# Keeping the second head group of a linear attention on chip, with VectorE sums and a new order of the seven products

## The chip, the cores and the metric

The kernel runs on one core of a Trainium2 chip. The metric is device time in microseconds (us) of one execution; lower is better. The engines have short names in the profile: PE is the matrix engine, PEld its weight loads, DVE the vector engine, ACT the scalar engine, POOL and SP the two engines that mostly issue DMAs here. Each engine works through its own instructions strictly in order and waits at semaphores for the others.

## What is computed

An input `x` of 2048 tokens by 512 goes through two branches, which a sigmoid gate mixes:

```python
g = sigmoid((x * gate_w).sum(-1))
# branch a: linear attention, 32 heads of 16
q, k, v = split(x @ wqkv)
pq, pk = phi(q), phi(k)          # phi(t) = (t+1 if t > 0 else exp(t)) + 1e-6
kv  = pk^T v      per head;   z = sum over tokens of pk
a = ((pq kv) / (pq z + 1e-6)) @ wo
# branch b: bilinear GLU, 1792 hidden columns
b = ((x @ w_gate) * (x @ w_up)) @ w_down
out = g * a + (1 - g) * b
```

## The kernel before

All matrices are float32. A product is made from three matmuls of rounded operands: `split` writes a high part (an ACT copy that rounds) and a low part (a DVE subtraction), and `mm3` adds high times high, high times low and low times high.

The first stage (to about 92 us) makes k, the sums over tokens, and per head block the small matrices kv. Then `kv` and `wo` are multiplied into one 512x512 matrix W', stored in DRAM in 256x256 blocks (`wraw`). So what the second stage calls **o** is the normalised `pq`, and branch a is o times W'.

The second stage runs over two **pairs** of token chunks (1024 tokens each). Each pair has 16 **units**: 14 for the hidden columns of branch b (`f`) and two for q (`q`), in the order f0 f1 f2 q f3 f4 f5 q f6 to f13 in the first pair and f0 q f1 f2 f3 q f4 to f13 in the second. They are counted through: units 0 to 15 and 16 to 31. A unit is a fast 2x2 block multiplication with seven products (products 2, 3, 4, 1, 5, 6, 7 in that order, six 512-wide matmuls each) into the PSUM banks Y, X, R and S. DVE and ACT combine the banks between the products (`bR`, `t`, `bS`, `cross`, `m`).

Between the products PE works off **down jobs** (h times `w_down`: six 512-wide matmuls each), as many at each of four places in a unit as the table `shares` says: after product 3, after product 4, after product 5, and before product 6. An entry `(0, 1, 0, 1)` gives one after product 4 and one before product 6. The first down job of each token tile is taken from PSUM by ACT (`acc<-att`, `acc<-dn`), the later ones by DVE.

Everything else is hung on named places of units with `later(n, place, fn)`: `e` (after product 3), `c` and `d` (after product 4), `t` (after product 1), `s` (after product 5), `r` (after product 6), `end` (after product 7). The order in which these calls run is the order on each engine, since every operation is pinned to program order.

**How o comes about.** A q unit makes one of two groups of heads (`j` = 0 or 1), in four parts of 128 rows by 512 tokens: row half r, token half c. `quad` writes phi(q) into a tile of the pool `ph`; the three units after that make the denominators, by way of DRAM (`terms`, `den`), and `norm_end` multiplies phi(q) by the scaled reciprocal that a broadcast DMA has put into a tile `rb` (pool `z`). `o_there` then stores the part to DRAM (`opark`), in a block named by group and token half: "11", "12", "21", "22".

**What is done with it.** `products` multiplies o by W' with seven block products (`OPROD`). Each entry holds: a number, the blocks of W' to be summed (one or two, a minus for a sign), the blocks of o to be summed, whether the product goes on in the PSUM bank of the one before, and which blocks of the result take it. Each product has two **steps** (one per half of the tokens); in the second pair the same seven products also take four units of branch b (`MIXED`, rows `hraw`), so that each has two steps for h and two for o. A step sits on one place: four per unit in the first pair, five in the second. Around step k, `load(k + 5)` fetches the first block of o from DRAM on SP's queue, `add(k + 3)` has POOL add the second block to it in a DMA (`dma_add`), after an ACT negation where the first has a minus, `ready(k)` splits the sum into the operands `oh` and `ol`, and `job(k)`, twelve 256-wide matmuls and one or two DVE sums into `acc`, follows in PE's order after the next down place. `w_raw`, `w_sum` and `w_split` do the same for the weights (`wraw`, `owh`, `owl`), and `lead` says how many steps ahead.

SP's queue holds, besides, the loads of the unit weights (`w_load`: `wr<-in_wgu`, for the unit three later) and of `w_down` (`wdr`), and waits at each until the buffer is free. POOL's queue holds the adding loads of the unit weights (`w_add`: `wr<-in_wgu_add`), which need ACT to have copied two parts of the tile first. During units 15 and 16 the operands of x for the second pair are reloaded one by one (`reload`): load after the last product that used them, for three of them a DMA add, then a split by ACT and DVE.

Operations recorded through the helpers have the helpers' lines: L72 matmuls, L78 ACT, L81 and L84 DVE, L102 DMAs of SP, L105 adding DMAs of POOL.

Of the kernel before, what the change touches and what calls it, by code (L numbers as in the profile page):

```python
# [49 lines left out]

OPROD = (
# [12 lines left out]
def gated_mix(ctx: ExitStack, tc, xt, xp, x, wqkv, wq, wq_add, wo, wgu, wgu_add, wdn, gate_w, out):  # L64
# [336 lines left out]
    def o_down():  # L401
        while ojobs and ojobs[0][0] < passed[0]:
# [154 lines left out]
    def wp_load():  # L557
        att["wv"] = two_by_two("wv")
        att["wo"] = [p2.tile([P, D], F32, tag="ph", name="wo_sb", bufs=4) for _ in range(KT)]
        for k in range(KT):  # L560
            dma(att["wv"][k], wqkv[k * P:(k + 1) * P, 2 * D:3 * D])
        for k in range(KT):
            dma(att["wo"][k], wo[k * P:(k + 1) * P, :])
# [91 lines left out]
    def down_jobs(pair, group):  # L655
# [3 lines left out]
        def job(i):  # L659
# [28 lines left out]
            if not todo[0]:  # L688
# [5 lines left out]

    opark = {(p, b): dram.tile([2, P, 2, HALF], F32, name=f"opark{p}{b}") for p in range(NPAIR)
             for b in ("11", "12", "21", "22")}

    def attention(pair, j, n):
        phs, den = {}, {}
# [4 lines left out]
        def quad(r, c, q):  # L704
# [3 lines left out]
            ph = phs[r, c] = p2.tile([P, CH], F32, tag="ph", name="phq", bufs=4)  # L708
# [42 lines left out]
        def norm_end(i):  # L751
            r, c = parts[i]
            stt(den[i], phs[r, c], EPS, den[i], ALU.add, ALU.mult)
            o_there(f"{j + 1}{c + 1}", r, den[i])
# [13 lines left out]
        if j == 1:  # L768
            products(pair, n + 5)
# [6 lines left out]
    def products(pair, n0):  # L776
        raw, tiles, wt, bank = {}, {}, {}, {}
        steps = STEPS[bool(MIXED[pair])]
        step0 = len(steps) * n0 + (1 if MIXED[pair] else 2)


        lead = ((6, 3), (5, 3)) if MIXED[pair] else ((4, 2), (4, 2))
# [5 lines left out]

        def raw_tile(k):
            raw[k] = p2.tile([P, D], F32, tag=("z", "ph")[k % 2], name="oraw", bufs=4)  # L790
            return raw[k]

        def load(k):
            p, kind, i = line[k]
            if kind == "o":
                dma(raw_tile(k).rearrange("p (r t) -> p r t", r=2), opark[pair, OPROD[p][2][0][-2:]][i])

        def add(k):
            p, kind, i = line[k]
            if kind == "o":  # L800
                if len(OPROD[p][2]) == 2 and OPROD[p][2][0][0] == "-":
                    act(raw[k], raw[k], scale=-1.0)
                for block in OPROD[p][2][1:]:
                    dma_add(raw[k].rearrange("p (r t) -> p r t", r=2), opark[pair, block][i])

        def h_sum(k):
            p, kind, r = line[k]
            if kind == "h" and len(OPROD[p][2]) == 2:
                one, other = OPROD[p][2]
                tt(raw_tile(k), row(other, r), row(one, r), ALU.subtract if one[0] == "-" else ALU.add)  # L810
# [7 lines left out]
        def w_raw(j):  # L818
            p, kind, _ = line[2 * j]
            tag = ("z", "ph")[p % 2] if kind == "h" else "cb"  # L820
# [14 lines left out]
        def ready(k, place):  # L835
            p, kind, i = line[k]
            tiles[k] = hi, lo = o_tiles()
            src = raw.pop(k) if k in raw else row(OPROD[p][2][0], i)
            if OPROD[p][2] == ("-22",):
                act(hi, src, scale=-1.0)  # L840
                stt(lo, src, -1.0, hi.bitcast(F32), ALU.mult, ALU.subtract)
            else:
                split(hi, lo, src)
# [40 lines left out]
        def weights(k, ahead, fn):  # L884

            for j in range(last // 2):
                if 2 * j - 1 - (ahead and lead[j % 2][ahead - 1]) == k:
                    at_step(k, lambda place, j=j: fn(j))

        for k in range(-8, last):  # L890
# [3 lines left out]
            if 0 <= k + 1 < last:  # L894
                at_step(k, lambda place, k=k: h_sum(k + 1))
            if 0 <= k + 3 < last:
                at_step(k, lambda place, k=k: add(k + 3))
            weights(k, 2, w_sum)
            if 0 <= k + 5 < last:
                at_step(k, lambda place, k=k: load(k + 5))  # L900
# [157 lines left out]
```

## Time and profile before

| what | value |
|---|---|
| time, median of 3 runs | 606.84 us (606.51 to 607.49) |
| the profiled execution's own time | 606.07 us |
| its span, first to last instruction | 604.4 us |
| PE busy | 595.6 us (99%) |
| DVE busy | 461.9 us (76%) |
| ACT busy | 331.9 us (55%) |
| POOL busy | 76.3 us (13%) |
| moved by DMA | 113.94 MB |

All times in the profile are us from the start of the span. A group row reads: line, engine, operation, what it writes and reads, shape, count; then busy time, the mean of one in ns, and the idle time ahead of it with what ended it. A row of the timeline reads: start, duration, engine, line, operation, and in brackets the idle time before it with its releaser. A row of a windows table gives, for a stretch of time, its length and each engine's busy time, then the granted share of the PE clock (1.00 is full), the busy share of the 16 DMA engines and GB/s. Matmuls are pipelined: one takes 0.39 us from start to end, but the next may start after 0.23 us.

### The profile page before, as it was taken

The numbers are of one execution on the slowest core, as the hardware profiler recorded it, in microseconds if no ns is written. First come the engines' busy times: TensorE is split into PE (matmuls) and PEld (weight loads), VectorE is DVE, ScalarE is ACT, GpSimd is POOL, SyncE is SP. The second block draws the span as 40 slices with busy tenths as digits, with TensorE's granted clock in tenths as the row PEclk, the third lists the DMA queues.
The fourth block names the chain that finished last, engine by engine and source line by source line (L and its number), as shares of the span: only waits on it lengthen the run. The fifth ranks groups of instructions, "written<-read, shape, count | busy, mean of one in ns | idle before, by whom it ended". The sixth has DMA issues, their size and how long they took to land.

```text
span 604.4 us, 8314 instructions
## 1 busy us (share of the span) xinstructions
PE 595.6 (99%) x2898; PEld 497.8 (82%) x2898; DVE 461.9 (76%) x736; ACT 331.9 (55%) x580; POOL 76.3 (13%) x95
## 2 busy tenths in 40 slices
PE   9999999999999999999999999998999999999997
PEld 6888888888888878888888888786888798888886
DVE  6977896756787769777789976866587887878866
ACT  3855766579654744445455648459543556246330
POOL 0011100000011110222011221000102412201100
PEclk9999999999999999999999999999999999999999
DMA  9576949656869877999679957877679987935103
GB/s 296 175 196 124 297 89 294 158 154 177 250 151 241 204 206 196 253 262 226 187 163 237 227 158 194 220 210 187 145 191 254 231 203 196 233 60 123 21 16 139
DMA packets 63626, 113.94 MB, mean 189 GB/s; under 512 B 7840, under 2 KB 27808, under 8 KB 63520
## 3 DMA queue, kind: packets, MB, share of 16 engines
q1 hardware_dynamic: 50640, 75.40, 38.2%
q0 software_dynamic: 12656, 37.49, 34.8%
q10 hardware_dynamic: 288, 0.52, 0.3%
q8 instruction: 22, 0.36, 0.2%
q14 instruction: 20, 0.16, 0.1%
HBM read 97.65 MB, written 17.84 MB: 191 GB/s over the span
## 4 chain that ended last, share of the span: by engine, by line
PE 83%; DMA 7%; DVE 5%; issue 2%; ACT 2%; SPq 0%; DVEq 0%; POOL 0%; ACTq 0%; POOLq 0%
PE dn L72 14%; PE att L72 13%; PE bY L72 12%; PE bR L72 11%; PE bX L72 11%; PE pk L72 7%; PE gt L72 7%; PE bS L72 6%; DMA wr<-in_wgu 2%; DMA wraw<-in_wdn 1%; DMA zt<-terms 1%; DMA wdr<-in_wdn 1%; DMA den<-den 1%; PE warm L72 1%; DMA rb<-den 1%
## 5 line engine op out<-in xcount | busy, mean ns | idle before, releaser
L72 PE MATMUL dn<-slot,slot 128*128 128x512 f32 (+1 forms) x336 | 83.0, 386 | 0.0
L81 DVE TENSOR_TENSOR wcl<-wr,wch 128x512 fp32r<-128x512 f32 (+1 forms) x96 | 73.6, 773 | 1.9 <-ACT wch L78 1.7
L78 ACT ACTIVATE slot<-cross 128x512 fp32r<-128x512 f32 x48 | 30.2, 629 | 80.9 <-DVE cross L81 80.9
L72 PEld LDWEIGHTS dn<-slot,slot 128*128 128x128 f32 x336 | 61.7, 188 | 12.1
L72 PE MATMUL att<-slot,slot 128*128 128x512 f32 x246 | 62.3, 390 | 0.0
L78 ACT ACTIVATE wch<-wr 128x512 fp32r<-128x512 f32 (+1 forms) x96 | 60.4, 695 | 1.6 <-DMA wr<-in_wgu_add 1.6
L72 PEld LDWEIGHTS att<-slot,slot 128*128 128x128 f32 x246 | 45.8, 188 | 9.3
L105 POOL DMA_DIRECT2D wr<-in_wgu_add x28 | 24.1, 860 | 219.1 <-ACT wr L78 146.0
L72 PE MATMUL bX<-xbh,wch 128*128 128x512 f32 x128 | 49.8, 389 | 0.0
L72 PE MATMUL bX<-xbh,wcl 128*128 128x512 f32 x128 | 49.8, 389 | 0.0
L72 PE MATMUL bX<-xbl,wch 128*128 128x512 f32 x128 | 49.8, 389 | 0.0
L78 ACT ACTIVATE cross<-bY 128x512 f32<-128x512 f32 x32 | 19.1, 597 | 50.4 <-PE bY L72 50.2
L81 DVE TENSOR_TENSOR t<-bR,cross 128x512 f32<-128x512 f32 x32 | 22.1, 690 | 26.0 <-PE bR L72 14.0
L78 ACT ACTIVATE wr<-wr 128x512 f32<-128x512 f32 x64 | 36.7, 623 | 6.2 <-DMA wr<-in_wq 3.3
L84 DVE SCALAR_TENSOR_TENSOR acc<-dn,gate,acc 128x512 f32<-128x512 f32 (+1 forms) x45 | 33.1, 737 | 9.1 <-PE dn L72 8.8
L78 ACT ACTIVATE cross<-bX 128x512 f32<-128x512 f32 x32 | 19.1, 597 | 33.5 <-DVE bS L81 33.5
L81 DVE TENSOR_TENSOR bR<-bX,m 128x512 f32<-128x512 f32 x32 | 22.3, 698 | 18.4 <-PE bX L72 17.2
L84 DVE SCALAR_TENSOR_TENSOR acc<-att,gate,acc 128x512 f32<-128x512 f32 x36 | 26.9, 749 | 11.8 <-PE att L72 11.6
L81 DVE TENSOR_TENSOR slot<-cross,slot 128x512 fp32r<-128x512 f32 x48 | 32.8, 684 | 0.5
L78 ACT ACTIVATE m<-bY 128x512 f32<-128x512 f32 x32 | 19.1, 595 | 24.5 <-PE bY L72 24.4
L105 POOL DMA_DIRECT2D oraw<-opark x20 | 19.7, 1037 | 91.2 <-ACT oraw L78 27.8
L72 PE MATMUL att<-owh,ol 128*128 128x256 f32 x100 | 28.6, 286 | 0.7 <-DVE ol L81 0.7
(191 smaller groups left out, 1586.6 us busy)
## 6 DMA issues: line engine op xcount, KB each, us to landing
wr<-in_wgu_add POOLq DMA_DIRECT2D x28, 640.0 KB, 6.8
wr<-in_wgu SPq DMA_DIRECT2D x28, 384.0 KB
oraw<-opark SPq DMA_DIRECT2D x28, 256.0 KB
wdr<-in_wdn SPq DMA_DIRECT2D x24, 256.0 KB
oraw<-opark POOLq DMA_DIRECT2D x20, 256.0 KB, 6.3
xraw<-in_x SPq DMA_DIRECT2D x16, 256.0 KB
terms<-zq SPq DMA_DIRECT2D x16, 256.0 KB
zt<-terms SPq DMA_DIRECT2D x16, 256.0 KB
```

The costliest lines, as they stand in the source:

```text
L72: tc.keep_in_program_order(nc.tensor.matmul(*args, **kw))
L78: pin(nc.scalar.activation(dst, src, func, **kw))
L81: pin(nc.vector.tensor_tensor(dst, a, b, op=op))
L84: pin(nc.vector.scalar_tensor_tensor(dst, a, scalar, b, op0=op0, op1=op1))
L105: tc.keep_in_program_order(nc.gpsimd.dma_start(dst, src, accum_op=ALU.add))
```

## The change

The blocks of the second group of heads ("21", "22") are no longer stored to DRAM: `norm_end` writes them in place over phi(q), and the tiles of pool `ph` stay with them until the last product has used them. For that `ph` holds two tiles of two rows where it held four of one, and the tiles for loaded or summed o (`oraw`) come from pool `z` alone. A sum of two blocks of which one or both are on chip is made by DVE (`on_chip`, one step ahead of `ready`); only the sum of "11" and "12" remains a DMA add. The negations by ACT go. A single block "-22" is split straight from the tile.

The seven products change their order, from 1, 6, 5, 7, 2, 4, 3 to 5, 7, 2, 1, 6, 4, 3. In the first pair all steps lie one unit sooner (steps 0 to 13 from unit 11 `t` to unit 14 `end`, before from unit 12 `t` to unit 15 `end`). Loads of o are issued three steps ahead (four where a DMA add follows, which comes two steps ahead), before five and three. In the second pair the first weight load leads by five steps, before by six or five by turns, and its tiles come from other pools. In `shares` a down job of unit 20 moves to unit 21, whose two now both lie after product 5 (one each after product 5 and before product 6), and in unit 26 one moves from after product 4 to after product 5.

By count this removes 8 stores of o, 8 loads of o, 16 adding DMAs and 8 ACT negations, and adds 16 DVE sums of 128x512. The matmuls are the same ones in another order.

```diff
--- before.py
+++ after.py
@@ -48,12 +48,13 @@
 
 
 
+
 OPROD = (
-    (1, ("11", "22"), ("11", "22"), False, (("11", 1),)),
-    (6, ("-11", "21"), ("11", "12"), True, (("22", 1),)),
     (5, ("11", "12"), ("-22",), False, (("12", -1),)),
     (7, ("-22", "12"), ("21", "22"), True, (("11", 1),)),
     (2, ("21", "22"), ("11",), False, (("21", 1), ("22", -1))),
+    (1, ("11", "22"), ("11", "22"), False, (("11", 1),)),
+    (6, ("-11", "21"), ("11", "12"), True, (("22", 1),)),
     (4, ("22",), ("-11", "21"), False, (("11", 1), ("21", 1))),
     (3, ("11",), ("-22", "12"), False, (("12", 1), ("22", 1))),
 )
@@ -407,9 +408,9 @@
 
     shares = {2: (0, 1, 1, 1), 3: (1, 0, 1, 0), 4: (1, 0, 1, 0), 7: (1, 1, 0, 1), 8: (1, 0, 1, 0), 9: (1, 1, 0, 1)}
     shares.update({units + m: v for m, v in ((0, (1, 2, 1, 2)), (1, (0, 1, 1, 0)), (2, (0, 1, 0, 0)),
-                                             (3, (0, 1, 0, 0)), (4, (0, 1, 0, 1)), (5, (0, 1, 0, 0)),
+                                             (3, (0, 1, 0, 0)), (4, (0, 1, 0, 0)), (5, (0, 0, 1, 1)),
                                              (6, (0, 1, 0, 1)), (7, (1, 1, 0, 0)), (8, (0, 1, 0, 1)),
-                                             (9, (1, 1, 0, 1)), (10, (0, 1, 0, 1)), (11, (0, 1, 0, 0)))})
+                                             (9, (1, 1, 0, 1)), (10, (0, 0, 1, 1)), (11, (0, 1, 0, 0)))})
 
     def share(n):
         return shares.get(n, (1, 1, 1, 1))
@@ -556,7 +557,8 @@
 
     def wp_load():
         att["wv"] = two_by_two("wv")
-        att["wo"] = [p2.tile([P, D], F32, tag="ph", name="wo_sb", bufs=4) for _ in range(KT)]
+        both = [p2.tile([P, 2, D], F32, tag="ph", name="wo_sb", bufs=2) for _ in range(KT // 2)]
+        att["wo"] = [both[k // 2][:, k % 2] for k in range(KT)]
         for k in range(KT):
             dma(att["wv"][k], wqkv[k * P:(k + 1) * P, 2 * D:3 * D])
         for k in range(KT):
@@ -692,11 +694,12 @@
         return [lambda i=i: job((i + TPP // 2) % TPP) for i in range(TPP)]
 
 
+
     opark = {(p, b): dram.tile([2, P, 2, HALF], F32, name=f"opark{p}{b}") for p in range(NPAIR)
-             for b in ("11", "12", "21", "22")}
+             for b in ("11", "12")}
 
     def attention(pair, j, n):
-        phs, den = {}, {}
+        both, phs, den = {}, {}, {}
 
         terms = dram.tile([2, KT, 2 * HB, DH, P], F32, name=f"terms{pair}{j}")
         there = dram.tile([2, 2 * HB, KT, P], F32, name=f"den{pair}{j}")
@@ -705,7 +708,9 @@
 
             ex = p2.tile([P, CH], F32, tag="z", name="ex", bufs=4)
             act(ex, q, AF.Exp)
-            ph = phs[r, c] = p2.tile([P, CH], F32, tag="ph", name="phq", bufs=4)
+            if c not in both:
+                both[c] = p2.tile([P, 2, CH], F32, tag="ph", name="phq", bufs=2)
+            ph = phs[r, c] = both[c][:, r]
             act(ph, q, AF.Relu)
             stt(ph, ex, 1.0, ph, ALU.min, ALU.add)
 
@@ -750,8 +755,11 @@
 
         def norm_end(i):
             r, c = parts[i]
-            stt(den[i], phs[r, c], EPS, den[i], ALU.add, ALU.mult)
-            o_there(f"{j + 1}{c + 1}", r, den[i])
+            if j:
+                stt(phs[r, c], phs[r, c], EPS, den[i], ALU.add, ALU.mult)
+            else:
+                stt(den[i], phs[r, c], EPS, den[i], ALU.add, ALU.mult)
+                o_there(f"1{c + 1}", r, den[i])
 
         for i in range(4):
             later(n + 1, "e", lambda i=i: z_part(i))
@@ -766,48 +774,61 @@
         for i, (m, place) in enumerate(((n + 3, "s"), (n + 3, "r"), (n + 3, "end"), (n + 4, "e"))):
             later(m, place, lambda i=i: norm_end(i))
         if j == 1:
-            products(pair, n + 5)
+            products(pair, n, both)
         return quad
 
 
 
     rows_of_h = {}
 
-    def products(pair, n0):
+    def products(pair, n, o_here):
         raw, tiles, wt, bank = {}, {}, {}, {}
         steps = STEPS[bool(MIXED[pair])]
-        step0 = len(steps) * n0 + (1 if MIXED[pair] else 2)
-
-
-        lead = ((6, 3), (5, 3)) if MIXED[pair] else ((4, 2), (4, 2))
+        step0 = len(steps) * (n + 5) + 1 if MIXED[pair] else len(steps) * (n + 4) + 2
+
+        lead = (5, 3) if MIXED[pair] else (4, 2)
 
         line = [(p, kind, i) for p in range(len(OPROD)) for kind in ("ho" if MIXED[pair] else "o") for i in range(2)]
 
         def row(block, r):
             return rows_of_h[pair, MIXED[pair][2 * (int(block[-2]) - 1) + r]][:, int(block[-1]) - 1]
 
+        def o_row(block, i):
+            return o_here[int(block[-1]) - 1][:, :, i * HALF:(i + 1) * HALF]
+
+        def two(t):
+            return t.rearrange("p (r t) -> p r t", r=2)
+
         def raw_tile(k):
-            raw[k] = p2.tile([P, D], F32, tag=("z", "ph")[k % 2], name="oraw", bufs=4)
+            raw[k] = p2.tile([P, D], F32, tag="z", name="oraw", bufs=4)
             return raw[k]
 
+        def parked(k, n):
+
+            p, kind, i = line[k]
+            blocks = [b for b in OPROD[p][2] if b[-2] == "1"] if kind == "o" else []
+            return opark[pair, blocks[n][-2:]][i] if n < len(blocks) else None
+
         def load(k):
-            p, kind, i = line[k]
-            if kind == "o":
-                dma(raw_tile(k).rearrange("p (r t) -> p r t", r=2), opark[pair, OPROD[p][2][0][-2:]][i])
+            if parked(k, 0) is not None:
+                dma(two(raw_tile(k)), parked(k, 0))
 
         def add(k):
-            p, kind, i = line[k]
-            if kind == "o":
-                if len(OPROD[p][2]) == 2 and OPROD[p][2][0][0] == "-":
-                    act(raw[k], raw[k], scale=-1.0)
-                for block in OPROD[p][2][1:]:
-                    dma_add(raw[k].rearrange("p (r t) -> p r t", r=2), opark[pair, block][i])
-
-        def h_sum(k):
+            if parked(k, 1) is not None:
+                dma_add(two(raw[k]), parked(k, 1))
+
+        def on_chip(k):
             p, kind, r = line[k]
-            if kind == "h" and len(OPROD[p][2]) == 2:
-                one, other = OPROD[p][2]
-                tt(raw_tile(k), row(other, r), row(one, r), ALU.subtract if one[0] == "-" else ALU.add)
+            blocks = OPROD[p][2]
+            if len(blocks) == 1 or parked(k, 1) is not None:
+                return
+            if kind == "h":
+                one, other = row(blocks[0], r), row(blocks[1], r)
+                tt(raw_tile(k), other, one, ALU.subtract if blocks[0][0] == "-" else ALU.add)
+                return
+            dst = two(raw[k] if k in raw else raw_tile(k))
+            one, other = [dst if b[-2] == "1" else o_row(b, r) for b in blocks]
+            tt(dst, other, one, ALU.subtract if blocks[0][0] == "-" else ALU.add)
 
         def w_block(p, kind, block):
             if kind == "o":
@@ -817,7 +838,7 @@
 
         def w_raw(j):
             p, kind, _ = line[2 * j]
-            tag = ("z", "ph")[p % 2] if kind == "h" else "cb"
+            tag = "z" if MIXED[pair] and j in (1, 2) else "cb"
             wt[j] = p2.tile([P, 2, HALF], F32, tag=tag, name="wraw", bufs=3 if tag == "cb" else 4)
             dma(wt[j], w_block(p, kind, OPROD[p][1][0]))
 
@@ -835,12 +856,18 @@
         def ready(k, place):
             p, kind, i = line[k]
             tiles[k] = hi, lo = o_tiles()
-            src = raw.pop(k) if k in raw else row(OPROD[p][2][0], i)
-            if OPROD[p][2] == ("-22",):
+            block = OPROD[p][2][0]
+            if k in raw:
+                split(hi, lo, raw.pop(k))
+            elif kind == "h" and block[0] != "-":
+                split(hi, lo, row(block, i))
+            else:
+                assert OPROD[p][2] == ("-22",)
+                src = row(block, i) if kind == "h" else o_row(block, i)
+                if kind == "o":
+                    hi, lo = two(hi), two(lo)
                 act(hi, src, scale=-1.0)
                 stt(lo, src, -1.0, hi.bitcast(F32), ALU.mult, ALU.subtract)
-            else:
-                split(hi, lo, src)
 
             ends = MIXED[pair] and k >= last - 2
             ojobs.append((LAST if ends else passed[0] - (place == "end"), lambda: job(k)))
@@ -884,7 +911,7 @@
         def weights(k, ahead, fn):
 
             for j in range(last // 2):
-                if 2 * j - 1 - (ahead and lead[j % 2][ahead - 1]) == k:
+                if 2 * j - 1 - (ahead and lead[ahead - 1]) == k:
                     at_step(k, lambda place, j=j: fn(j))
 
         for k in range(-8, last):
@@ -892,12 +919,13 @@
             if k >= 0:
                 at_step(k, lambda place, k=k: ready(k, place))
             if 0 <= k + 1 < last:
-                at_step(k, lambda place, k=k: h_sum(k + 1))
-            if 0 <= k + 3 < last:
-                at_step(k, lambda place, k=k: add(k + 3))
+                at_step(k, lambda place, k=k: on_chip(k + 1))
+            if 0 <= k + 2 < last:
+                at_step(k, lambda place, k=k: add(k + 2))
             weights(k, 2, w_sum)
-            if 0 <= k + 5 < last:
-                at_step(k, lambda place, k=k: load(k + 5))
+            for m in (3, 4):
+                if 0 <= k + m < last and m == (3 if parked(k + m, 1) is None else 4):
+                    at_step(k, lambda place, k=k + m: load(k))
             weights(k, 1, w_raw)
```

## The prediction

> **What bounds the kernel now.** I read the page's table of busy times first, then the waits of PE, then windows cut at the units that the change touches, then the timelines of PE, ACT, SP and POOL around each wait.
>
> ```profile
> PE 595.6 (99%) x2898; PEld 497.8 (82%) x2898; DVE 461.9 (76%) x736; ACT 331.9 (55%) x580; POOL 76.3 (13%) x95
> ```
>
> PE is busy for 595.6 of 604.4 us. So the end is set by the number of matmuls, which the change leaves alone, and by some 9 us in which PE stands. What a change of order can win is in those 9 us; what it can lose has no such limit.
>
> ```profile
> PE bY L72 <- ACT m L78: 2.0, 1, 2.0
> PE warm L72 <- DVE xc1h L128: 1.3, 1, 1.3
> PE att L72 <- ACT oh L78: 0.8, 1, 0.8
> ```
>
> A row gives the engine and tile that wait, the one waited for, the sum, how often, and the longest. The second is the start, the third is a wait for an operand of o: this the change can reach. The first is a wait of branch b, in unit 22, whose surroundings `shares` changes.
>
> Windows: length, then busy PE, PEld, DVE, ACT, POOL with counts, clock, DMA share, GB/s. They are units 13, 15, 16, 25 to 27 in part, 28 to 30 in part, and 30 with the start of 31.
>
> ```profile
> 271.00:292.00 21.00, 21.00 (x116) 18.30 (x115) 16.54 (x26) 9.60 (x19) 4.32 (x5) 1.00 0.95 213
> 312.00:333.00 21.00, 21.00 (x117) 18.30 (x116) 19.87 (x32) 12.23 (x21) 3.40 (x4) 1.00 0.89 225
> 333.00:353.00 20.00, 19.82 (x92) 16.09 (x91) 18.55 (x25) 11.43 (x17) 4.29 (x6) 1.00 0.90 218
> 452.00:490.00 38.00, 36.66 (x183) 30.60 (x182) 29.34 (x46) 17.77 (x32) 10.79 (x11) 1.00 1.03 244
> 480.00:540.00 60.00, 60.00 (x345) 52.99 (x344) 47.35 (x75) 30.93 (x56) 10.27 (x11) 1.00 0.79 184
> 540.00:580.00 40.00, 40.00 (x228) 35.20 (x227) 33.36 (x53) 17.33 (x31) 3.41 (x4) 1.00 0.31 62
> ```
>
> DVE has 1.1 us left in unit 15 (19.87 of 21.00); the DMA engines are full around unit 26 (1.03). Elsewhere both have room.
>
> **The change, part by part.** The matmuls are the same ones in another order: 0.
>
> *First pair one unit sooner.* Units 11 to 14 take the work that 12 to 15 had, so DVE's fullest unit loses it. PE shows what that unit costs at its end (rows of tile `att`):
>
> ```profile
> 335.92 0.28 PE L72 MATMUL att<-owh,oh 128*128 128x256 f32 x1
> 336.04 0.28 PE L72 MATMUL att<-owl,oh 128*128 128x256 f32 x1
> 336.50 0.39 PE L72 MATMUL att<-owh,ol 128*128 128x256 f32 x1 [0.18 <-DVE ol L81]
> 336.72 0.28 PE L72 MATMUL att<-owh,oh 128*128 128x256 f32 x1
> ```
>
> Two 256-wide matmuls start 0.12 apart (335.92, 336.04). The three up to 336.72 took 0.80 instead of 0.36. This job now runs in unit 15, at a DVE that no longer does four steps of o: −0.44, between −0.44 and 0.
>
> *The reload of x,* in units 15 and 16, comes later against its users: four jobs of o (twelve times 0.12, 1.42 us each) leave unit 15, which therefore starts 5.7 us later and ends at the same time. Its last tile:
>
> ```profile
> 339.56 0.85 POOL L105 DMA_DIRECT2D xal<-xnext  x1 [0.41 <-PE dn L72]
> 349.47 1.05 ACT L78 ACTIVATE xah<-xal 128x1024 fp32r<-128x1024 f32 x1
> DMA to landing us min/median/max: 8.3/8.3/8.3
> ```
>
> Issued at 339.56 it lands at 347.9, and ACT comes to it at 349.47: 1.6 us to spare. I estimate that it is issued 1.3 later, as POOL gets there in the queue; the two adds of o (of four) that go from this stretch, with a DMA share of 0.90, give some of that back. So it stays hidden, just: +0.2, between 0 and +2.5 (if nothing is given back and the two tiles ahead slip with it).
>
> *`shares`, units 20 and 21.* Moving down jobs moves no matmul time, but each first job of a token tile takes ACT along. Rows of ACT (two of tile `acc`, then two of the chain ahead of `m`), of SP, and of PE:
>
> ```profile
> 397.78 0.68 ACT L78 ACTIVATE acc<-att,gate 128x512 f32<-128x512 f32 x1
> 405.58 0.69 ACT L78 ACTIVATE acc<-dn,gate 128x512 f32<-128x512 f32 x1 [0.76 <-PE dn L72]
> ```
> ```profile
> 409.51 1.15 ACT L78 ACTIVATE wr<-wr 128x512 f32<-128x512 f32 x2 [0.83 <-DMA wr<-in_wgu]
> ...
> 415.04 0.62 ACT L78 ACTIVATE m<-bY 128x512 f32<-128x512 f32 x1
> ```
> ```profile
> 401.41 0.66 SPq L102 DMA_DIRECT2D wr<-in_wgu  x1
> ```
> ```profile
> 413.31 0.39 PE L72 MATMUL bX<-xbh,wcl 128*128 128x512 f32 x1
> 415.72 0.50 PE L72 MATMUL bY<-xc4h,wch 128*128 128x512 f32 x1 [2.02 <-ACT m L78]
> ```
>
> From 409.51, when the weights that SP fetched at 401.41 have landed, ACT works without a gap to `m`, and PE stands 2.02 us for it. The two `acc` copies lay before that, where ACT was idle next. After the change both come behind the copy `wr<-wr` in ACT's order, inside the gapless chain; SP's issue stays behind the stores of the first group, which remain. Two copies, 0.58 apart in a row of such, push `m` and PE: +1.16. It is 0 if the weights land 1.2 sooner, +1.16 if not; nothing else in the chain moves. I take +1.16, since the issue at 401.41 stays where it is.
>
> *Unit 26, the second pair's first jobs of o.* PE:
>
> ```profile
> 472.18 0.32 PE L72 MATMUL att<-owh,oh 128*128 128x256 f32 x1
> ...
> 473.42 0.28 PE L72 MATMUL dn<-owh,oh 128*128 128x256 f32 x1
> ...
> 474.13 1.55 PE L72 MATMUL dn<-slot,slot 128*128 128x512 f32 x6
> 476.50 0.39 PE L72 MATMUL att<-owh,oh 128*128 128x256 f32 x1 [0.81 <-ACT oh L78]
> ...
> 477.88 0.28 PE L72 MATMUL dn<-owh,oh 128*128 128x256 f32 x1
> ```
>
> Six matmuls of 256 take 0.71: 472.18 to 473.42 lost 0.53, 476.50 to 477.88 lost 0.67. The six of 512, 0.23 apart, take 1.36: 474.13 to 476.50 lost 1.01. In all 2.2. What came late was the summed weight:
>
> ```profile
> 460.42 1.51 POOL L105 DMA_DIRECT2D wraw<-in_wdn  x1
> ```
> ```profile
> DMA to landing us min/median/max: 9.0/9.5/10.0
> ```
> ```profile
> 469.44 0.63 ACT L78 ACTIVATE owh<-wraw 128x512 fp32r<-128x512 f32 x1 [2.69 <-DMA wraw<-in_wdn]
> ```
> ```profile
> 471.44 0.63 ACT L78 ACTIVATE oh<-oraw 128x512 fp32r<-128x512 f32 x1 [0.87 <-DVE oraw L81]
> ```
>
> It landed 9.0 us after its issue, at full DMA engines; ACT had stood 2.69 for it and then 0.87 more for DVE's sum of the operand. The changed kernel leaves out stores of the second group, loads and adds of o in this stretch, and its first product takes "-22" straight from the tile, with no DVE sum ahead of `oh`. The missing 0.87 alone is worth 0.9, since ACT has no further gap up to the `oh` for which PE stood; if the weight also lands 1.5 to 2 sooner, all but the small waits for `ol` goes. So −2.0, between −0.9 and −2.2. What is late next is `ol` of the second step, at DVE, for some 0.2.
>
> [...]
>
> *DVE sums in place of DMAs.* A row of tile `oraw` (shortest, median and longest in ns):
>
> ```profile
> L81 DVE TENSOR_TENSOR oraw<-hraw x10: 683/686/689, 470.7 to 573.8; 128x512 f32<-128x512 f32 x10
> ```
>
> Sixteen sums of 0.686 are 11.0 us of DVE; eight ACT negations, sixteen POOL adds, eight stores and eight loads of SP go. A unit of the first pair gets at most four sums: in unit 13 DVE comes to 16.54 + 2.74 = 19.3 of 21.0, 92%, below the 95% at which unit 15 lost 0.44. The second pair gets two a unit: 47.35 + 3.8 in 60 us is 85%, 33.36 + 2.5 in 40 is 90%. The sums stand a step ahead of their split, about 5 us, so PE covers them: 0, between 0 and +3.4 (five of them on the path). Without that cover each would cost 0.69. SP's queue gets shorter, and group two has no landing left to wait for; nothing is gained by either away from unit 26, as PE waits for no load of o there now.
>
> **The sum.** −0.44 + 0.2 + 1.16 − 2.0 + 0 = −1.1 on the profiled execution's 606.07 us (span 604.4), which is 0.77 below the median. From the median of 606.84 that gives 605.8.
>
> **Rivals.** *B, more is won.* The lighter queues let the weights of unit 22 land 1.2 sooner, so the two copies find ACT idle again. For it speaks that group two is stored no more; against it that SP issues at 401.41 in both. −2.24: 604.6.
>
> *C, DVE becomes the bound: slower.* In units 12 to 14 or 28 to 30 (92%, 90%) the sums collide with the banks' combinations, which come in bursts. It decides when the second sum reaches PE (1.4 us against the 1.1 won); with five, 3.4 − 1.1 = +2.3: 609.1. For it speaks unit 15 at 95%, against it that PE lost only 0.44 there.
>
> *D, the reload of x comes late: slower.* With the whole +2.5 in place of 0.2 the sum is +1.2: 608.0. It begins at 1.6 us of delay, and loses from 1.3 us of standing on. Against it stands the smaller load of the DMA engines in just this stretch.
>
> *E, the clock drops.* The gap ahead of product 4 in unit 22 grows from 2.0 to 3.2 us. A cold PE shows at the start:
>
> ```profile
> 1.26 3.59 PE L72 MATMUL warm<-xc1h 128*128 128x512 bf16 x8 [1.26 <-DVE xc1h L128]
> ```
>
> Eight matmuls in 3.59 instead of 8 × 0.23 = 1.82: +1.8, so 607.5. Against it stands the page's row of the granted clock in 40 slices, full in the 28th too (408 to 423 us), where the gap of 2.02 lies:
>
> ```profile
> PEclk9999999999999999999999999999999999999999
> ```
>
> [...]
>
> *F, unit 26 keeps its stall,* because ACT's order (`owh` behind copies of unit weights) holds it and not the landing: with only the 0.9 the sum is 0, 606.8; with nothing +0.9, 607.7.
>
> **How the numbers follow.** Forecast 0.43 (own range 604.8 to 606.8: the bounds of unit 26 and of the first term), B 0.17, C 0.15, D 0.12, E 0.04, F 0.09. Some 0.2% (1.2 us) is what a measurement can tell from no change. The forecast lies just inside: 0.19 of it faster, 0.24 same. B is faster. C, half of D (it lies at the edge) and 0.01 of E make slower 0.22; the rest is same: 0.36, 0.42, 0.22. The range goes from 604.2, a little below B, to 608.6, which takes in D, E, F and the near half of C.
>
> **What would show it.** Right: PE's wait for `oh` near 477 gone or below 0.3; the wait for `m` in unit 22 at 3.2; `xah` split by 350.5 without a wait for its DMA; no new row of PE waiting for `ol` above 0.3 in units 11 to 14. Wrong: PE standing for `bS` or `ol` in units 12 to 14 and 28 to 30 (C), or for `xah` near 351 (D); a clock below 1.00 behind unit 22 (E); ACT still waiting for `wraw` over 2 us (F); the wait for `m` at 2.0 (B).

## The result and the profile after

The changed kernel takes 615.09 us (611.18 to 616.22), the kernel before in the same comparison 607.16: a ratio of 1.0117 (95% interval 1.0067 to 1.0166). A second measurement, in a later session, gave 613.9 us and 1.0097 (1.0060 to 1.0135). The prediction was 605.8 us, with 608.6 as the upper end: wrong in sign. The profiled execution took 614.29 us, its span is 612.3 against 604.4.

Ratios below compare runs of one session; ratios, not medians, are carried from session to session, as the kernel before itself ran between 605.2 and 612.0 us in these. A few executions that were several times as long or, on one chip, 50 us longer are left out of the ratios, and the profiles of two of them are not read.

Busy times of the page, after:

```profile
PE 598.6 (98%) x2898; PEld 499.4 (82%) x2898; DVE 470.9 (77%) x752; ACT 328.4 (54%) x572; POOL 62.4 (10%) x79
```

The same 2898 matmuls, but 3.0 us more of PE time. DVE has 16 instructions more and 9 us more, POOL 16 fewer: the change does what it says. The waits of PE, after:

```profile
PE att L73 <- ACT oh L79: 3.8, 2, 3.1
PE bY L73 <- ACT m L79: 1.4, 1, 1.4
PE warm L73 <- DVE xc1h L129: 1.3, 1, 1.3
PE bR L73 <- DVE bR L82: 1.0, 1, 1.0
PE bS L73 <- DVE xal L82: 0.8, 1, 0.8
PE att L73 <- DVE ol L85: 0.5, 2, 0.3
PE bS L73 <- ACT xah L79: 0.3, 1, 0.3
PE bY L73 <- DVE xc4l L82: 0.3, 1, 0.3
PE bR L73 <- DVE xc1l L82: 0.3, 1, 0.3
```

The longest, 3.1 us for `oh`, is at a place where the kernel before had no wait: the first job of o in the first pair, now in unit 11. PE's timeline there:

```profile
250.78 0.84 PE L73 MATMUL dn<-slot,slot 128*128 128x512 f32 x3
254.68 0.39 PE L73 MATMUL att<-owh,oh 128*128 128x256 f32 x1 [3.06 <-ACT oh L79]
...
256.00 0.42 PE L73 MATMUL att<-owl,oh 128*128 128x256 f32 x1
256.22 0.41 PE L73 MATMUL att<-owh,ol 128*128 128x256 f32 x1
...
257.71 0.63 PE L73 MATMUL bR<-xc6h,wch 128*128 128x512 f32 x1
```

Behind the wait the 256-wide matmuls start 0.22 apart and not 0.12. The windows (clock in the third column from the right) tell why:

```profile
251.00:254.00 3.00, 0.62 (x3) 0.19 (x1) 2.55 (x4) 3.00 (x6) 0.00 (x0) 1.00 0.36 63
254.00:258.00 4.00, 3.09 (x13) 2.89 (x14) 3.26 (x6) 1.23 (x3) 1.73 (x2) 0.67 0.54 81
258.00:262.00 4.00, 4.00 (x17) 3.23 (x17) 3.04 (x5) 1.41 (x3) 0.00 (x0) 0.90 1.03 209
```

The granted clock is 0.67 and 0.90 behind the wait, in which stretches of full and half clock are averaged (the trace has it at 0.50 from 255.36 to 258.77). In all PE lost 5.3 us here: 3.2 of standing, some 1.6 by the half clock, and the rest in short waits. Why `oh` is late, on SP, POOL and ACT:

```profile
230.28 2.58 SPq L103 DMA_DIRECT2D rb<-den  x4
232.95 0.59 SPq L103 DMA_DIRECT2D wdr<-in_wdn  x1
233.59 0.43 SPq L103 DMA_DIRECT2D xsum<-cbs  x1
234.06 0.43 SPq L103 DMA_DIRECT2D wraw<-wraw  x1
```
```profile
246.59 0.85 POOL L106 DMA_DIRECT2D wraw<-wraw  x1 [11.70 <-DMA wraw<-wraw-22_95]
```
```profile
250.67 0.63 ACT L79 ACTIVATE owh<-wraw 128x512 fp32r<-128x512 f32 x1 [4.87 <-DMA wraw<-wraw]
251.21 1.87 ACT L79 ACTIVATE wch<-wr 128x512 fp32r<-128x512 f32 x3
252.98 1.13 ACT L79 ACTIVATE wr<-wr 128x512 f32<-128x512 f32 x2
254.02 0.61 ACT L79 ACTIVATE oh<-phq 128x512 fp32r<-128x512 f32 x1
```

The first weight load stands in SP's queue behind the four broadcasts of the denominators and two more transfers. Issued at 234.06, it is added to only at 246.59 (the row names the next weight load as releaser; but the add waits for the semaphore of its own load too, and by that semaphore's updates in the trace the load was complete only at 246.1, 12.0 us after its issue). The sum lands 4.1 us later, ACT has waited 4.87, and five copies of unit weights stand between `owh` and `oh` in ACT's order. One unit later, in the kernel before, the first weight load came behind no broadcasts: issued at 245.86, 13 us behind the last of them, it was complete at 250.3 by its semaphore's updates, 4.5 us after its issue.

Time that PE lost against its usual distance from one matmul to the next (0.23 for 512, 0.12 for 256 wide), summed from the two timelines by place:

| place | before | after |
|---|---|---|
| first job of o, unit 11 (half clock included) | 0 | 5.3 |
| operands of x, unit 16 | 0.3 | 2.8 |
| units 21 and 22 | 2.3 | 3.0 |
| unit 26 | 2.2 | 1.6 |
| last job of o of the first pair | 0.45 | 0 |
| rest (start among it) | 4.1 | 4.1 |
| sum | 9.3 | 16.8 |

That is 7.5 of the 7.9 us by which the span grew.

### The profile page after: what moved, and what is told of

It is laid out like the page before. It is cut to its first block, busy times and chain, and to the rows that moved or that the text cites. A ratio compares the mean times of both kernels' runs of the same rounds, so it can differ in the third digit from the quotient of the medians.

```text
span 612.3 us, 8234 instructions
## 1 busy us (share of the span) xinstructions
PE 598.6 (98%) x2898; PEld 499.4 (82%) x2898; DVE 470.9 (77%) x752; ACT 328.4 (54%) x572; POOL 62.4 (10%) x79
## 4 chain that ended last, share of the span: by engine, by line
PE 83%; DMA 8%; DVE 4%; ACT 3%; issue 2%; SPq 0%; ACTq 0%; DVEq 0%; POOLq 0%
PE dn L73 14%; PE att L73 13%; PE bR L73 12%; PE bY L73 12%; PE bX L73 11%; PE pk L73 7%; PE gt L73 7%; PE bS L73 6%; DMA xc6l<-xnext 2%; DMA wraw<-in_wdn 1%; DMA wraw<-wraw-22_95 1%; DMA wr<-in_wgu 1%; DVE wcl L82 1%; DMA rb<-den 1%; DMA wraw<-wraw 1%
## 5 line engine op out<-in xcount | busy, mean ns | idle before, releaser
L73 PE MATMUL dn<-slot,slot 128*128 128x512 f32 x336 | 84.5, 390 | 0.0
L73 PE MATMUL att<-slot,slot 128*128 128x512 f32 (+1 forms) x246 | 60.8, 384 | 0.0
L85 DVE SCALAR_TENSOR_TENSOR acc<-dn,gate,acc 128x512 f32<-128x512 f32 x45 | 33.6, 749 | 10.0 <-PE dn L73 9.6
L82 DVE TENSOR_TENSOR bR<-bX,m 128x512 f32<-128x512 f32 x32 | 22.3, 697 | 16.8 <-PE bX L73 15.7
L73 PE MATMUL att<-owh,oh 128*128 128x256 f32 x104 | 29.9, 288 | 3.8 <-ACT oh L79 3.8
L85 DVE SCALAR_TENSOR_TENSOR acc<-att,gate,acc 128x512 f32<-128x512 f32 (+1 forms) x36 | 26.3, 733 | 9.2 <-PE att L73 9.2
L73 PE MATMUL att<-owh,ol 128*128 128x256 f32 x104 | 30.2, 291 | 0.5 <-DVE ol L85 0.5
```

What stands on the lines that cost most here:

```text
L73: tc.keep_in_program_order(nc.tensor.matmul(*args, **kw))
L82: pin(nc.vector.tensor_tensor(dst, a, b, op=op))
L85: pin(nc.vector.scalar_tensor_tensor(dst, a, scalar, b, op0=op0, op1=op1))
```

## The experiments

**The place undone.** The first pair's products go back by one unit, all else stays changed.

```diff
-        step0 = len(steps) * (n + 5) + 1 if MIXED[pair] else len(steps) * (n + 4) + 2
+        step0 = len(steps) * (n + 5) + (1 if MIXED[pair] else 2)
```

> The changed kernel with one part undone: the first pair's products of o lie one unit later, as before (units 12 to 15). Theory Q (the place): the 5.3 us around 251 us (PE waits 3.2 for oh, then 2.1 at the half clock) come from the first weight load standing in SP's queue behind four broadcasts, and the 2.5 us for the operands of x from a shorter unit 15; both come from the earlier place, so both go: 606.3 to 607.5 us, clock 1.00, no wait of PE for oh in the first pair above 0.5. Rival S (the sums on chip and the new order of products): both stay wherever the steps lie, 611 us or more.

Measured 1.0017 (0.9995 to 1.0039). The same kernel once more, for a profile:

> The same kernel as the one with the first pair's products one unit later, for an undisturbed profile beside its time. Theory Q (the place): no wait of PE for oh above 0.5 us in units 12 to 15, waits for x operands in unit 16 together below 0.4; what is left against before is units 21 and 22 (2.8 us against 2.2) and unit 26 (1.6 against 2.2). Time equal to before within 0.3%. Rival S: a wait of 2 us or more for oh at the first job, at 0.5% or more above before.

Measured 1.0005 (0.9983 to 1.0028). PE's waits from 240 to 360 us, which cover the first pair's products and unit 16:

```profile
PE att L73 <- ACT oh L79: 0.8, 1, 0.8
PE att L73 <- DVE ol L82: 0.3, 1, 0.3
```

No wait in unit 12 and none for x: theory Q holds, both losses belong to the earlier place, not to the sums of DVE or the order of products. The 0.8 is at the last job of the pair; "none above 0.5" was not met there, and PE lost 1.65 us at that job, against 0.45 before: at this place the rest of the change is not free either.

**Only the first weight earlier.** The place stays one unit sooner; the first load goes ahead of the broadcasts, and its add one step ahead of its old place.

```diff
+        first = lead if MIXED[pair] else (7, 3)
...
-                if 2 * j - 1 - (ahead and lead[ahead - 1]) == k:
+                if 2 * j - 1 - (ahead and (first if j == 0 else lead)[ahead - 1]) == k:
```

> The changed kernel, with only the first weight load and its adding DMA of the first pair issued earlier (load in unit 9 ahead of the broadcasts, add in unit 10 after product 1). Theory Q: the wait near 251 us and the low clock behind it go, 5.3 us, and the 2.5 us of the x reload stay: 609.0 us with a clock of 1.00. Rival S: the operand oh is late for DVE's or ACT's sake and not for the load, so nothing changes: 613 to 615 us.

Measured 1.0032 (1.0010 to 1.0053). PE has no wait at all from 240 to 300 us: of the 1.2% lost (1.0 in the second measurement), 0.65 to 0.85 come from the place of one load and its add in their queues. The expected clock of 1.00 did not come: its profile, with a wait of 2.3 us for `m` in unit 22, had 0.997, as one stretch of 3.41 us at half clock gives. The waits for x stayed (3.2 us, counted as in the table).

**The load from POOL's queue.**

```diff
+    def dma_pool(dst, src):
+        tc.keep_in_program_order(nc.gpsimd.dma_start(dst, src))
...
-            dma(wt[j], w_block(p, kind, OPROD[p][1][0]))
+            (dma if j or MIXED[pair] else dma_pool)(wt[j], w_block(p, kind, OPROD[p][1][0]))
```

> The changed kernel, with the first weight load of the first pair issued by POOL at its old place and not by SP; its add stays. Theory Q (the order in SP's queue: the load waits behind four broadcasts that use half of the DMA engines): the load lands in 3 to 6 us, the add is issued by 241 and PE's wait for oh at the first job falls from 3.1 us to below 0.5, the clock behind it stays at 1.00: 609 us or 0.9% less than the changed kernel. Rival E (the DMA engines themselves are full from 237 to 246, whatever the queue): the load still lands near 245 and the wait stays at 2.5 or more.

Measured 1.0023 (0.9999 to 1.0046), no wait above 0.2 at the first job. POOL, with the landing of the first and the second `wraw` row:

```profile
226.12 0.89 POOL L106 DMA_DIRECT2D wraw<-wraw  x1
236.35 0.86 POOL L109 DMA_DIRECT2D wr<-in_wgu_add  x1 [9.34 <-DVE wcl L82]
236.91 1.18 POOL L109 DMA_DIRECT2D wraw<-wraw  x1
```
```profile
DMA to landing us min/median/max: 6.7/6.7/6.7
```
```profile
DMA to landing us min/median/max: 12.1/12.1/12.1
```

POOL came to the load 8 us earlier than SP had, ahead of the broadcasts, so this does not separate the queue from the full DMA engines (in the changed kernel their busy share was 0.42 to 0.59 from 232 to 236 us and 0.95 to 1.18 from 236 to 243). The add, issued behind the broadcasts, took 12.1 us on the other queue; but there it also stood behind the 640 KB of `wr<-in_wgu_add`, which in the changed kernel took 11.1 at this place (median 6.4). So landings were late on both queues, as rival E said, and which share belongs to the neighbour is not shown. What helped was to issue the load ahead of the broadcasts.

**A longer unit 15.** As the kernel with the early first weight, and two down jobs moved from unit 14 to 15.

```diff
-    shares = {2: (0, 1, 1, 1), 3: (1, 0, 1, 0), 4: (1, 0, 1, 0), 7: (1, 1, 0, 1), 8: (1, 0, 1, 0), 9: (1, 1, 0, 1)}
+    shares = {2: (0, 1, 1, 1), 3: (1, 0, 1, 0), 4: (1, 0, 1, 0), 7: (1, 1, 0, 1), 8: (1, 0, 1, 0), 9: (1, 1, 0, 1), 14: (1, 0, 1, 0), 15: (1, 2, 1, 2)}
```

> As the kernel with the early weight load, and in addition two down jobs (2.7 us of PE) move from unit 14 to unit 15, which gets longer by that. Theory W (the reload of x has too little time in a unit 15 of 16.4 us): the waits of PE for xc1l, xah and xal in unit 16 fall from 2.5 to below 1, 607 us. Rival T (the reload is late because the DMA engines are full, whatever the length): the waits stay near 2.5, 609 us.

Measured 1.0003 (0.9982 to 1.0025), 0.3% less than without. But the loss at the waits for x in its profile only fell from 3.2 to 2.2 us; in the kernel with everything mended below, which is the same up to unit 20, no such wait is above 0.2. In four profiles with the short unit 15 the loss was 2.5 to 3.2. So the length helps, by an amount that varies between executions.

**The table of down jobs alone, on the kernel before.**

```diff
-                                             (3, (0, 1, 0, 0)), (4, (0, 1, 0, 1)), (5, (0, 1, 0, 0)),
+                                             (3, (0, 1, 0, 0)), (4, (0, 1, 0, 0)), (5, (0, 0, 1, 1)),
...
-                                             (9, (1, 1, 0, 1)), (10, (0, 1, 0, 1)), (11, (0, 1, 0, 0)))})
+                                             (9, (1, 1, 0, 1)), (10, (0, 0, 1, 1)), (11, (0, 1, 0, 0)))})
```

> The kernel before with one part of the change alone: the new table of down jobs in units 20, 21 and 26. The prediction's term: two copies of acc come into ACT's gapless chain ahead of m, PE's wait in unit 22 grows from 2.0 to 3.2, +1.2 us: 608.0. By the changed kernel's profile (waits of 2.8 in units 21 and 22 against 2.2) it is +0.6: 607.4. Rival: the weights land earlier and hide both, 606.8.

Measured 1.0023 (0.9998 to 1.0047), +1.4 us, just not clear of zero. In its profile the long wait is not for `m` in unit 22 (0.3 us) but for `bR` in unit 21:

```profile
404.28 0.80 PE L72 MATMUL bR<-xc1h,wch 128*128 128x512 f32 x1 [2.13 <-DVE bR L81]
404.88 0.63 PE L72 MATMUL bR<-xc1l,wch 128*128 128x512 f32 x1
```

With a down job less in unit 20, PE comes to product 1 of unit 21 before DVE, which has waited for the broadcasts of the denominators, has made `bR`. Here too half clock follows (matmuls of 0.63, starting 0.42 apart). The same profile lost 4.7 us in unit 26, whose entry also changed, against 2.2 in the first profile of the kernel before; so the +1.4 is not that of units 20 and 21 alone.

**The second pair's first weight one step earlier,** on the kernel with the later place:

```diff
+        first = (6, 4) if MIXED[pair] else lead
...
-                if 2 * j - 1 - (ahead and lead[ahead - 1]) == k:
+                if 2 * j - 1 - (ahead and (first if j == 0 else lead)[ahead - 1]) == k:
```

> As the kernel with the products one unit later, and the second pair's first weight load and its adding DMA one step earlier (six and four steps ahead, before five and three). Theory L (the landing of the summed weight sets the stall of unit 26): ACT no longer waits 2.6 us for it, PE's waits for oh and ol there fall from 1.6 us to below 0.4, 1.3 us less than the kernel without it. Rival O (ACT's order, owh and oh behind five copies of unit weights): the wait of PE stays at 1.2 or more.

Measured 0.9986 (0.9964 to 1.0008), against 1.0005 without. Unit 26 is read from the profile of the next kernel, which has the same edit and also the old entries for units 20 and 21.

> As the kernel before this in the list, with the old table of down jobs in units 20 and 21 (unit 26 keeps the new one). Prediction's term: 1.2 us less than with the new table; by the profiles 0.6 less. Together with unit 26 cured 0.2 to 0.4% below the kernel before. Rival: no difference between the two tables, as the wait for m in unit 22 stays at 2 us or more.

Measured 0.9953 (0.9933 to 0.9973): faster than the kernel before, and 0.33% or 2.0 us less than with the new entries (expected: 1.2, or 0.6 by the profiles). ACT comes to the weight of unit 26 without waiting, and from 465 to 480 us PE has one listed wait:

```profile
466.72 0.62 ACT L79 ACTIVATE owh<-wraw 128x512 fp32r<-128x512 f32 x1
```
```profile
PE att L73 <- DVE ol L85: 0.3, 1, 0.3
```

PE loses 0.9 us there, with 2.0 in the kernel one unit later without the edit: theory L in the main, though "below 0.4" was too much to ask.

**The same edit alone, on the kernel before.**

```diff
-                if 2 * j - 1 - (ahead and lead[j % 2][ahead - 1]) == k:
+                if 2 * j - 1 - (ahead and ((6, 4) if MIXED[pair] and j == 0 else lead[j % 2])[ahead - 1]) == k:
```

> The kernel before with one edit alone: the adding DMA of the second pair's first weight is issued one step earlier (four ahead, before three). Theory L (the landing of the weight sets unit 26's stall, whatever happens to o): PE's waits there fall from 2.2 to below 1, 606.9 us or 0.2% less than before, so that o on chip is worth nothing by itself. Rival N (o on chip is needed: the DVE sum and the loads of o hold the step as well): the waits stay at 1.8 or more, as before.

Measured 0.9954 (0.9936 to 0.9973): as much as the best kernel with o on chip. POOL's rows and the landing of the first:

```profile
459.94 1.20 POOL L105 DMA_DIRECT2D wraw<-in_wdn  x1 [13.21 <-DVE wcl L81]
460.66 1.43 POOL L105 DMA_DIRECT2D wr<-in_wgu_add  x1
```
```profile
DMA to landing us min/median/max: 7.1/7.1/7.1
```

The add stands 0.5 us earlier in its span than before, but 1.1 us later against the `m` that ACT makes next (464.03, before 465.64). What changed is the order: it goes ahead of the 640 KB of unit weights and not behind them, and lands after 7.1 us and not 9.0. ACT still waited 1.94 us for it (2.69 before), and PE's loss in unit 26 fell only from 2.2 to 1.7, so by PE's waits neither theory's figure is met; the time says more than this profile explains.

**Where the kernel before loses that.** The gain of 2.7 us is more than the 0.5 of the profile. Three further profiles of the kernel before:

> The kernel before again, for a profile of another execution. Theory H: where its clock is at 0.997 or below, the half clock lies behind unit 26 (two or three waits of PE within 5 us, 2.2 us in all, now longer), and so the early weight of unit 26 takes it away. Theory G22: it lies behind the wait of 2.0 us or more for m in unit 22, and the early weight has nothing to do with it.

The second and third had the same expectation. The first and third had a clock of 0.997, at 610.35 and 610.69 us; the second 0.999, at 607.2. The third, in unit 26:

```profile
476.63 0.39 PE L72 MATMUL att<-owh,oh 128*128 128x256 f32 x1 [2.42 <-ACT oh L78]
...
478.66 2.75 PE L72 MATMUL dn<-slot,slot 128*128 128x512 f32 x6
```

In both the first job waits for `oh` in one piece (1.9 and 2.4 us), the longest wait of its profile. In the third half clock follows 2 us later: the six matmuls take 2.75 us, where they took 1.55 in the row quoted for the prediction. In the first no other wait is above 1.4 us, and the clock of 0.997 is that of one stretch too. Theory H: in these two the half clock sits behind unit 26, in the first by its waits alone. Of 103 runs of the kernel before in three sessions 54 had a clock of 0.997 or less, as one stretch of 3.4 us at half clock in 606 us gives (median 608.68 us, the others 607.27); with the earlier weight one of twelve had. This does not account for the whole gain: in that session the 16 runs of the kernel before with a higher clock had a median of 607.64 us, and the eleven with the earlier weight 605.39. So some 2.2 us lie between executions without half clock; in unit 26 the profiles without it show only 0.5 to 0.8 of that (2.2 and 2.5 us lost before, 1.7 with the edit). Where the rest lies stays open.

**How long a wait costs the clock.** On the best kernel, two or five superfluous ACT copies ahead of `m` in unit 22:

```diff
+        for _ in range(2 if n == 22 else 0):
+            act(m2, xc[2][1].bitcast(F32)[:, 0])
         act(m2, bank["Y"])
```

> As the best kernel so far (products one unit later, early weight in unit 26, old table in units 20 and 21), with two more ACT copies ahead of m in unit 22, whose result is overwritten: PE stands some 1.1 us longer there, 2.7 us in place of 1.6. Theory G (the PE clock drops to half behind a gap of somewhat over 2 us): in most runs a clock of 0.997 or less, eight matmuls at 0.43 us behind the gap, +1.1 + 1.6 = 608.3 us. Rival (such a gap costs only its length): +1.1, 606.7 us, clock 1.00.

> The same with five copies: PE stands some 4.3 us. Theory G: every run shows a clock of 0.997 or less, +2.7 + 1.6 to 2 = 610.1 us. Rival: +2.7, 608.3 us, clock 1.00.

Without copies the wait was 1.43 us and none of ten runs had a clock of 0.997 or less. With two, PE, from its profile:

```profile
417.45 0.50 PE L73 MATMUL bY<-xc4h,wch 128*128 128x512 f32 x1 [2.77 <-ACT m L79]
...
418.56 0.63 PE L73 MATMUL bY<-xc4h,wch 128*128 128x512 f32 x1
418.99 0.63 PE L73 MATMUL bY<-xc4l,wch 128*128 128x512 f32 x1
```

Seven of ten runs had it, at 608.05 to 610.24 us; the other three took 605.49 to 606.47. Median 608.1, ratio 0.9988 (0.9964 to 1.0012). With five copies the wait is

```profile
419.00 0.80 PE L73 MATMUL bY<-xc4h,wch 128*128 128x512 f32 x1 [4.55 <-ACT m L79]
```

and all ten had it: 610.6 us, 1.0047 (1.0024 to 1.0070). Theory G, but the length of the wait does not decide alone: in the profile with the table of down jobs alone the 2.13 us for `bR` were followed by half clock, and a wait of 2.2 us for `oh` was not (its clock of 0.997 is that of one stretch). In the changed kernel's trace the half clock lasts 3.413 us; it begins 249.17 us, 73 times 3.413, after the first rise of the clock, and the next change comes 354.99 us, 104 times 3.413, after its end. In that of the kernel before 600.75 us, 176 times 3.413, lie between the rise and the next change. Cut at this step, counted from the rise (at 6.18 and 5.49 us), the changed kernel's unit 11 and the 2.02 us wait of the kernel before, which half clock did not follow, look like this:

```profile
251.95:255.35 3.40, 0.50 (x2) 0.30 (x2) 2.62 (x6) 2.68 (x5) 0.94 (x2) 1.00 0.05 9
255.36:258.76 3.40, 3.35 (x13) 3.16 (x14) 3.32 (x6) 0.60 (x1) 0.77 (x1) 0.50 0.87 144
258.78:262.18 3.40, 3.40 (x16) 2.79 (x16) 2.44 (x4) 1.59 (x3) 0.00 (x0) 1.00 1.03 218
```
```profile
411.68:415.08 3.40, 2.02 (x9) 1.32 (x8) 2.76 (x4) 3.40 (x8) 0.32 (x1) 1.00 0.72 104
415.09:418.49 3.40, 2.77 (x12) 2.32 (x13) 1.89 (x3) 3.40 (x7) 0.00 (x0) 1.00 0.78 219
```

The wait of the kernel before falls into two of these stretches, with 1.55 and 0.75 us lost (counted as in the table); that of the changed kernel lies mostly in one, with 3.2 lost. In these two traces, from the rise to the last matmul, the clock halved behind that stretch alone, and the others at full clock had lost 1.55 us at most. That the loss within one stretch decides is my estimate from these 3.2 and 1.55 us; no run tests it by itself. What the runs show is a chance that grows with the wait in the profile: none of ten at 1.43 us, seven at 2.77, ten at 4.55.

**Everything mended at the earlier place.** Early first weights in both pairs, longer unit 15, old entries for units 20 and 21: the edits above together.

> The changed kernel with its places kept (first pair one unit sooner) and everything mended that was found: early weight loads in both pairs, a longer unit 15, the old table in units 20 and 21. Theory Q (the earlier place costs through the reload of x only, 2.0 us, once the first load is early, and gains the 1.6 of the first job in unit 16): within 0.1% of the best kernel so far, 606.0 us. Rival: the sums of DVE in units 11 to 14 show up now, 608 us or more.

Measured 0.9960 (0.9943 to 0.9977), and PE waits for no operand of x: theory Q. The earlier place is neither better nor worse once its transfers are early and unit 15 is longer. Beside the kernel before with the early second weight alone, measured in the same session at 0.9954, neither place shows a gain from o on chip.

**The changed kernel again.**

> The changed kernel again, beside the kernel before on the same chip. The wait for oh near 251 us is back at 2.5 us or more with the half clock behind it in more than half of the runs, the x operands late by 2 us or more in unit 16; 0.8 to 1.5% slower than before.

All came back: a wait of 2.3 us for `oh` in unit 11 (expected: 2.5 or more), half clock behind it, 2.5 us for x, 1.0097; and half clock a second time, behind 2.2 us in unit 22 (the clock is 0.993, with one stretch it would be 0.997).

## Why the prediction was wrong, by its own steps

*Matmuls, 0.* Right in number; but PE was busy for 3.0 us more, some 1.6 of it by the half clock in unit 11.

*First pair one unit sooner, −0.44.* This step failed. The wait that it saw, at the pair's last job, did go. But it priced the move at its end alone. At its start the first weight load came to stand behind four broadcasts in SP's queue, the add behind that, and ACT behind both: 3.2 us of standing, 1.6 of half clock and some short waits, +5.3 in place of −0.44. The early load and add alone take it away, and with it 0.65 to 0.85 of the 1.0 to 1.2%.

*Reload of x, +0.2 of up to +2.5.* The upper end: +2.5. POOL's last add came 2.3 and not 1.3 later against unit 16, as the same loads were squeezed into a unit of 16.4 us, and DMA had less to move but less time. Yet the tile that the prediction watched, `xal`, still landed 1.0 us before ACT came to it (355.7 and 356.72). The tile ahead of it was late:

```profile
353.27 1.06 ACT L79 ACTIVATE xc6h<-xc6l 128x1024 fp32r<-128x1024 f32 x1 [1.56 <-DMA xc6l<-xnext]
```

DVE waited for that split, so `bS`, ACT's next copy and the split of `xah` behind it slipped too. Rival D by mechanism, with 0.12, by way of the tiles that the bound of +2.5 had named.

*`shares`, +1.16.* The size is not settled: +0.7 in the first two profiles, +1.4 by time for the whole table on the kernel before, 2.0 for the two entries on the kernel one unit later. The mechanism was wrong: `m` was not waited for longer; PE, now earlier, met `bR` that was late. That the size lies near is luck.

*Unit 26, −2.0 of −0.9 to −2.2.* Measured −0.6 in the first two profiles. The jobs there are the steps of the first product for h, not for o (ACT's row is `oh<-hraw` in the kernels with the change), so what the change took away is one sum, by the new order of products. The landing did not come sooner: 8.9 us after its issue, behind the same `wr<-in_wgu_add`, against 9.0 before.

```profile
467.54 0.85 POOL L106 DMA_DIRECT2D wr<-in_wgu_add  x1 [11.04 <-DVE t L82]
468.08 1.54 POOL L106 DMA_DIRECT2D wraw<-in_wdn  x1
```

I had laid the 9.0 to the traffic of o; with that traffic gone it stayed, and with the add ahead of its neighbour in POOL's own queue it was 7.1.

*DVE's sums, 0.* +0.35 (one short wait in unit 28): inside its range, and rival C did not happen.

*Rival E, the clock.* Right as a mechanism, at the wrong place, and with the wrong bound. I took one quiet execution as evidence that a wait of 2.0 us is harmless and gave it 0.04. Here half clock followed waits of 1.9, 2.1, 2.2, 2.3, 2.4 and 2.8 us, so the profiles decide against 2.0 us as a safe length.

## What to carry to other kernels

When steps move, price the move at both ends: look at what each queue holds at the new place of the *first* load, not only at what is relieved at the old place of the last. A transfer that is late in a row of the trace may be late for its neighbour in its own queue (here an add took 9.0 us behind 640 KB and 7.1 ahead of them); the cheapest test is to issue it ahead of that neighbour, and here one such edit gained the 0.46% that taking 32 transfers of o off the chip's memory did not, though the profiles locate only a part of it. One profile of a kernel with waits of 2 us and more shows one of two outcomes (with 2.77 us seven of ten runs had half clock and three had not); several runs' clocks show the other.

## What the runs showed of the hardware

Half clock after short waits: in the changed kernel's unit 11 it lasted 3.41 us, in which 256-wide matmuls start 0.22 and not 0.12 us apart, and 1.6 us were lost on top of the wait; with the two copies 512-wide matmuls start 0.43 and not 0.23 us apart. A wait of some 2 us brought it or not: 1.9 us in one profile of the kernel before (clock 0.997, its longest wait) and 2.13 with the table of down jobs alone came with it, 2.02 in the first profile of the kernel before and 2.2 with the table alone did not. With 1.43 us in the profile none of ten runs had it, with 2.77 seven, with 4.55 all ten.

Around four broadcasts of 256 KB, issued within 2.6 us, landings were late on both queues: in the changed kernel the load of 256 KB issued 1.2 us behind the last on SP's queue took 12.0 us, and the 640 KB add on POOL's 11.1 (median 6.4); an add of 256 KB issued 14 us behind the last took 4.1. How much of this the broadcasts cause, and how much the 640 KB, no run separates.
